# Attention in front of a mixture of experts: score banks with fixed owners, rows turned by two engines, and weight splits one chunk later

## Chip, core and metric

One core of a Trainium2 chip. The metric is the device time of one execution in microseconds; the time before is the median of three runs. Engines are called by their names in the profile: PE (TensorE; PEld its weight loads), DVE (VectorE), ACT (ScalarE), POOL (GpSimd) and SP (SyncE, which here only issues transfers).

## What is computed

Attention over 4 batches of 12 heads, 448 tokens and 64 columns a head, with a tanh cap on the scores; its output, as 1792 rows of 768, goes to a mixture of 8 experts with one expert for each row.

```python
scores = cap * np.tanh(scale * np.matmul(q, k.transpose(0, 1, 3, 2)) / cap)
scores = scores - np.max(scores, axis=-1, keepdims=True)
attn = np.exp(scores)
attn = attn / (np.sum(attn, axis=-1, keepdims=True) + 1e-09)
x = np.matmul(attn, v)                 # -> (1792, 768)
logits = x @ w_gate; e_idx = np.argmax(logits, axis=1)
eom = 1.0 / (1.0 + np.exp(-(x @ w_output_gate)))
for e in range(8):
    mask = e_idx == e
    ye = np.maximum(x[mask] @ w1[e], 0.0) @ w2[e]
    out[mask] = gate_w[mask, None] * eom[mask, e, None] * ye
```

## The kernel before

**Units.** Attention runs over 24 units `u`, six for each batch; a unit is two heads (j = 0, 1, head p and head p + 6). The code is written in the order in which each engine shall work (a manual schedule), so an engine takes its instructions strictly in that order, and the framework adds only the waits. For each unit PE makes the transposed scores in three full tiles of 128 tokens for both heads and a fourth, `s3`, that holds the last 64 tokens of both heads (`qk`). Each is a sum of three products, since Q and K are split in a high plane (`QH`, `K0H` to `K4H`) and a low one (`QL`, `K0L` ...). ACT puts a tanh over each tile (L398) and one exponential over the unit (`expo`, L401). One unit later PE multiplies by V (`pv`, L409, tile `u`), and ACT, or DVE in the first eight units, copies the result to SBUF as `ut` (`u_evac`).

**Sums.** POOL adds the four score tiles (`presum`, tile `pb`); every second unit PE multiplies these by a column of ones (`sums`, L441, tile `sm`).

**K and Q.** SP loads them in blocks of 32 columns; DVE turns the blocks with its 32x32 transpose (`turned`, L290) into a PSUM bank `tk`, and makes the planes by a cast (L280) and a difference (L286). `TURN` says how many of these steps are written before and after the rest of a unit's work; they run about three units ahead of their use. K's last 64 tokens of both heads are split by two extra casts and differences each.

**Banks.** Two banks of PSUM go to transposes and sums. The other six are a ring of three tiles of two banks (`scores`, `half`); whatever PE needs next, a score tile, `u`, or a small product, takes the next one of the three and waits until its last reader is done.

**End of a batch.** `end_of_batch` spreads the work on a finished batch over slots of the units behind it: the gate products (`gate_mm`, tile `tg`), the reciprocals of the sums (`sums_tr`, `recips`), the rows of x (`row_tr` on PE, tile `trow`; `row_out` on DVE, which multiplies by the reciprocals), the choice of the expert and the row's place in the expert's table (`logits`, `choose`, `rank_mm`, `place`, `place2`, `enter`). SP stores the rows (`store_rows`), POOL scatters the table entries. Slot names: "f" and "g" stand behind the unit's scores, "h" behind its exponential, "q" behind pv, "e" at its end.

**Hand-over.** While the last batch is still being finished, `two1` and `two2` start with two blocks of rows that share one expert's weights (`mm_two`): `split_to` splits each weight chunk (`raw`) in a high plane by ACT (L1069) and a low one by DVE (L1070), a fixed number of chunks ahead of PE's use, and then issues the load of the chunk that takes its place. `fetch_dma` loads a block's table rows (`tc`), `gather` fetches its rows of x (`xg`), and `tx` turns them on PE (`pt_x`).

Of the kernel before, what the change touches and what calls it, by code (L numbers as in the profile page):

```python
# [22 lines left out]
def tile_kernel(ctx: ExitStack, tc, q, k, v, cap, w_gate, w_ogate, w1, w2, out):  # L23
# [26 lines left out]
    for i, kind in enumerate((2, 4)):  # L50
# [8 lines left out]
    TURN = {0: (0, 0), 1: (0, 0), 3: (2, 1), 5: (2, 1), 6: (2, 1), 7: (2, 1), 9: (2, 1), 10: (1, 0), 11: (1, 0), 13: (2, 1),  # L59
            14: (2, 1), 15: (2, 1), 17: (1, 0), 20: (1, 0), 21: (0, 0), 22: (0, 0)}  # L60
# [47 lines left out]
    def load_natural(dst, src, n, m, engs):  # L108
        for j in range(2):
            engs[j].dma_start(out=dst[:, 0:n, j], in_=src[j, 0:n * m].rearrange("(c p) d -> p c d", c=n))  # L110

    def load_nat(u, engs):
        (k0, q0), k_, q_ = nat[u], heads(k, u), heads(q, u)
        load_natural(k0, k_, NK, 128, engs)
        engs[1].dma_start(out=k0[0:64, NK], in_=k_[:, SK:S].rearrange("j p d -> p j d"))
        load_natural(q0, q_, NCH, CP, engs)

    def load_pair(src, u, tiles, to):
        t = raw1[tiles[u // 2 % 3]][:, 0:2 * S].rearrange("p (h r a) -> p h r a", h=2, a=32)
        lo = u % 2  # L120
        for c in range(4):
            x = c % 2
            h = c // 2 * NP + u % NP
            nc.sync.dma_start(
                out=t[32 * c:32 * c + 32, lo:].rearrange("p h r a -> p (h r) a"),
                in_=src[u // NP, h:h + 2 - lo, :, 32 * x:32 * x + 32].rearrange("h (r b) a -> b (h r) a", b=32))
        for i in range(lo, 2):
            to[u + i - lo] = t[:, i]

    def load_k(u):  # L130
        load_pair(k, u, (0, 1, 4), ldk)

    def load_q(u):
        load_pair(q, u, (2, 3, 5), ldq)

    def v_main(u, eng):
        load_natural(vvs[u // 2 % 2][:, u % 2], heads(v, u), NK, 128, (eng, eng))

    def v_tails(u, eng):
        for j in range(2):  # L140
            h = j * NP + u % NP
            eng.dma_start(out=vvs[u // 2 % 2][64 * j:64 * j + 64, :, NK, j],
                          in_=v[u // NP, h:h + 2, SK:S].rearrange("h p d -> p h d"))
# [43 lines left out]
    for hl in kpl:  # L187
        for t in hl:
            nc.vector.memset(t.bitcast(F32)[0:64, SK + 64:], 0.0)
            nc.vector.memset(t.bitcast(F32)[64:128, SK:SK + 64], 0.0)  # L190
    for u in range(1, NN):
        load_nat(u, (nc.sync, nc.sync))
# [3 lines left out]
    ohc = rtp.tile([128, NP, 32], F32, name="ohc")  # L196
# [58 lines left out]
    def late_consts():  # L255
        nc.vector.memset(ohc, 0.0)
        for p in range(NP):
            nc.vector.memset(ohc[:, p, p:p + 1], 1.0)
# [29 lines left out]
    def turned(src, n):  # L288
        ps = tbank([128, n], "tk")
        nc.vector.transpose(out=ps, in_=src.rearrange("p r a -> p (r a)"))  # L290
        return ps
# [41 lines left out]
    def t_k(u):  # L333
        pl[u] = planes_of(k_parts(u, turned(ldk.pop(u), S)))
# [39 lines left out]
    def nat_q(u):  # L374
        pq = scores("tq0")[:, 0, 0:S]
        for c in range(NCH):
            nc.tensor.transpose(pq[:, c * CP:(c + 1) * CP], nat[u][1][:, c].rearrange("p j d -> p (j d)"), ident[0:CP, 0:CP])
        return pq

    def qk(u, s):  # L380
        KH, KL, QH, QL = pl[u]
        if s == 0:
            pt[u] = ptp.tile([128, 2 * NK + 1, S], F32, tag="pt", name="pt")
        n = 2 if s < NK else 1
        sl = slice(s * 128, (s + 1) * 128)
        if s < NK:
            ps = scores("s")
            for i, (x, y) in enumerate(((KH, QH), (KL, QH), (KH, QL))):
                for j in range(2):
                    h = slice(64 * j, 64 * j + 64)  # L390
                    nc.tensor.matmul(ps[:, j, 0:S], lhsT=x[h, sl], rhs=y[h], start=(i == 0), stop=(i == 2))  # L391
            ps = ps[:, :, 0:S]
        else:
            ps = half("s3")[:, 0:S]
# [8 lines left out]
    def pv(u, c):  # L403
        P = pt[u]
        V = vvs[u // 2 % 2][:, u % 2]
        if c == 0:
            ups[u] = half("u")[:, 0:S]
# [24 lines left out]
    def sums(u):  # L432

        b, p = divmod(u, NP)
        if p % 2 == 0:
            return
        r = p // 2
        if r == 0:
# [21 lines left out]
    def end_of_batch(b):  # L460
        def bank(shape, name, m=False):
# [4 lines left out]
            x = half(name)[0:shape[0], 0:math.prod(shape[1:])]  # L466
# [5 lines left out]
        def sums_out():  # L472
            ssb = T("ssb", [128, S])
            nc.scalar.activation(out=ssb, in_=smt.pop(b), func=ACTF.Copy)
# [7 lines left out]
        def recips():  # L482
            r = T("rec", [CP, NCH, NP // 2, 4])
            nc.vector.tensor_scalar(out=r.rearrange("p c n j -> p c j n"), in0=rt["trec"][:, :, :, 0:NP // 2],
                                    scalar1=epsc[0:CP], scalar2=None, op0=ALU.add)
            nc.vector.reciprocal(out=r, in_=r)
# [25 lines left out]
        def gate_mul(g):  # L512
            if g == 0:
                T("gm", [CP, NCH, H, 16])
            for i in range(2):
                c = 2 * g + i
                nc.vector.tensor_tensor(
                    out=rt["gm"][:, c], in0=rt["pg"][:, i].rearrange("p (h e) -> p h e", h=H),
                    in1=rec[b][:, c].unsqueeze(2).to_broadcast([CP, H, 16]), op=ALU.mult)

        def logits():
            l = T("lg", [CP, NCH, 16])
# [3 lines left out]
            d = T("d")  # L526
            nc.vector.tensor_tensor(out=d, in0=l[:, :, 0:E], in1=mx.unsqueeze(2).to_broadcast(sh), op=ALU.subtract)

        def choose():

            d = rt["d"]
            cand = T("cand")
            stt(cand, d, 0.0, ALU.is_lt, iota8[0:CP], ALU.add)
            fi = T("fi", [CP, NCH])
# [4 lines left out]
            nc.vector.tensor_tensor(out=og, in0=ohb, in1=rt["lg"][:, :, E:2 * E], op=ALU.mult)  # L539
# [17 lines left out]
        def place():  # L557
            ohb, ps = rt["ohb"], rt["ps"]
            rk = T("rk")
# [6 lines left out]
        def place2():  # L566
            rk = rt["rk"]
            nc.vector.tensor_tensor(out=rk, in0=rk, in1=rt["ohb"], op=ALU.mult)
            nc.vector.tensor_reduce(out=posi, in_=rk, axis=AX.X, op=ALU.max)

        def enter():

            den = rt["den"]
            nc.vector.tensor_reduce(out=den[:, 0], in_=rt["ex"], axis=AX.X, op=ALU.add)
            nc.vector.tensor_scalar(out=den[:, 1], in0=den[:, 1], scalar1=1.0, scalar2=None, op0=ALU.add)
            stt(den[:, 0], den[:, 0], 1e-9, ALU.add, den[:, 1], ALU.mult)
# [37 lines left out]

        L = lambda *fs: (lambda: [f() for f in fs])
        P = lambda f, *a: (lambda: f(*a))
        rws = [L(P(row_tr, p), P(row_out, p)) for p in range(NP)]
# [3 lines left out]
        if b < B - 2:  # L621
            at = {(-2, "q"): [g0], (0, "q"): [g1], (0, "e"): [sums_out], (1, "g"): [t[1]],
                  (2, "g"): [rws[0], rws[1]], (3, "g"): gts, (3, "h"): [logits], (4, "g"): [rws[2], rws[3]], (4, "h"): [choose],
                  (5, "g"): [rank_mm, place, rws[4]], (5, "h"): [place2, enter], (6, "g"): [rws[5]]}
            for i, x in enumerate(((6, "g"), (8, "g"), (9, "g"), (10, "g")) if b == 0 else ((6, "g"),) * NCH):
                at.setdefault(x, []).append(P(scatter, (i,)))
        elif b == B - 2:
# [7 lines left out]
                  (2, "q"): [fd[0], *lds[:2], fd[1]],  # L635
# [342 lines left out]
    for u in range(NU):  # L978
        if u % 2 and u < NU - 3:
            load_v(u + 1)  # L980
        for s in range(NK):
            qk(u, s)
# [4 lines left out]
        else:  # L987
            qk(u, NK)
# [127 lines left out]
    def mm_two(ps, which, acts, n, lag, done):  # L1116
# [250 lines left out]
```

## Time and profile before

| what | value |
|---|---|
| median of 3 runs | 509.56 us (508.12 to 510.07) |
| profiled execution | 510.44 us, span of its instructions 508.8 us |
| mean granted clock of PE | 0.993 |
| PE busy | 488.6 us (96%) |
| DVE busy | 383.0 us (75%) |
| ACT busy | 371.4 us (73%) |
| POOL busy | 286.8 us (56%) |

The busy share is a mean over stages: attention up to about 192 us, where all engines work, the end of the last batch and the first expert blocks up to about 240, and the experts behind them. Matmuls are pipelined and their ends are modelled, so PE's busy share overstates its work; what it waits for is read from the rows of one place in time.

### The profile page before, as it was taken

The page shows a single profiled execution, that of the slowest core. Times are in us where ns is not written, and L with a number is a line of the kernel's source. Part 1 is how long each engine was busy: PE and PEld are TensorE (multiplying, and loading weights), DVE is VectorE, ACT ScalarE, POOL GpSimd, SP SyncE. Part 2 cuts the span into 40 slices and gives each one's busy share as a digit, 9 for nine tenths or more (in the row PEclk, how much of TensorE's full clock was granted, in tenths as well). Part 3 has the DMA queues.
Part 4 walks back from the last instruction along what each step waited for, and adds up shares of the span by engine and source line. Part 5 has one row for each costly group of instructions (what it writes and reads, how often), then busy time and mean ns, then how long its engine had stood idle before and what let it go on. Part 6 is the DMA issues. An engine that isn't in the chain of part 4 may idle for free. (4 is left out here: it accounts for less than half of the span.)

```text
span 508.8 us, 9997 instructions
## 1 busy us (share of the span) xinstructions
PE 488.6 (96%) x3064; PEld 342.2 (67%) x3064; DVE 383.0 (75%) x746; ACT 371.4 (73%) x433; POOL 286.8 (56%) x310
## 2 busy tenths in 40 slices
PE   8999999999999999899999999999999999999994
PEld 6544445454544443678989979978788867686691
DVE  6789998889887879698989868866677947555550
ACT  5999998888978797356688968867677856674551
POOL 7899998698988614562259771237274144522001
PEclk9999999999999999899999999999999999999998
DMA  7879877476431449872199235279679599791001
GB/s 174 138 130 162 154 134 139 89 134 107 78 62 38 83 120 327 301 224 104 26 390 406 82 114 214 63 274 366 219 249 402 200 395 409 215 379 42 1 33 50
DMA packets 152379, 91.92 MB, mean 181 GB/s; under 512 B 135026, under 2 KB 135162, under 8 KB 152320
## 3 DMA queue, kind: packets, MB, share of 16 engines
q1 hardware_dynamic: 142336, 58.24, 42.8%
q0 software_dynamic: 8832, 32.74, 17.7%
q8 instruction: 26, 0.43, 0.3%
q10 hardware_dynamic: 1152, 0.25, 0.2%
q14 instruction: 33, 0.27, 0.2%
HBM read 123.68 MB, written 12.04 MB: 267 GB/s over the span
## 5 line engine op out<-in xcount | busy, mean ns | idle before, releaser
L1070 DVE TENSOR_TENSOR wr<-raw,wr 128x768 fp32r<-128x768 f32 (+1 forms) x167 | 171.9, 1067 | 66.5 <-ACT wr L1069 65.7
L1069 ACT ACTIVATE wr<-raw 128x768 fp32r<-128x768 f32 (+1 forms) x167 | 150.7, 935 | 30.9 <-PE py L1091 15.2
L398 ACT ACTIVATE pt<-s,icap 128x896 f32<-128x896 f32 x96 | 79.9, 913 | 11.0 <-PE s L391 10.8
L409 PE MATMUL u<-pt,vv 128*64 128x448 f32 x384 | 77.5, 546 | 1.4 <-ACT pt L398 1.1
L1091 PE MATMUL py<-wr,hh 128*128 128x384 f32 x352 | 77.3, 341 | 0.0
L1091 PE MATMUL php<-wr,xh 128*128 128x512 f32 x264 | 74.8, 405 | 0.0
L1160 POOL DMA_INDIRECT out_dram<-yo,ti x13 | 21.4, 1648 | 94.5 <-ACT yo L1158 71.3
L401 ACT ACTIVATE pt<-pt,capc 128x3136 f32<-128x3136 f32 x24 | 69.9, 2912 | 0.6
L1091 PEld LDWEIGHTS py<-wr,hh 128*128 128x128 f32 x352 | 61.2, 188 | 4.0 <-issue 3.7
L1091 PEld LDWEIGHTS php<-wr,xh 128*128 128x128 f32 x264 | 47.4, 188 | 12.8 <-issue 2.8
L409 PEld LDWEIGHTS u<-pt,vv 128*64 128x64 f32 x384 | 25.4, 136 | 41.3 <-issue 33.0
L417 POOL TENSOR_TENSOR pb<-pt 128x896 f32<-128x896 f32 x20 | 42.3, 2116 | 14.1 <-ACT pt L401 4.4
L422 POOL TENSOR_TENSOR pb<-pb,pt 64x448 f32<-64x448 f32 x40 | 45.7, 1142 | 3.1
L1091 PE MATMUL py<-wr,hl 128*128 128x384 f32 x176 | 44.8, 335 | 0.0
L418 POOL TENSOR_TENSOR pb<-pb,pt 128x896 f32<-128x896 f32 x20 | 42.0, 2100 | 1.6
L1091 PE MATMUL php<-wr,xl 128*128 128x512 f32 x132 | 41.6, 396 | 1.0 <-DVE xl L886 1.0
L1207 POOL DMA_DIRECT2D rh<-in_moe_w_dram x42 | 23.2, 555 | 16.6 <-DVE wr L1070 8.9
L1091 PEld LDWEIGHTS py<-wr,hl 128*128 128x128 f32 x176 | 31.8, 188 | 0.0
L1091 PEld LDWEIGHTS php<-wr,xl 128*128 128x128 f32 x132 | 24.7, 188 | 7.3 <-DVE xl L886 1.4
L290 DVE STREAM_TRANSPOSE tk<-raw 128x448 f32<-128x448 f32 x42 | 27.5, 655 | 0.9
L585 POOL DMA_INDIRECT tab<-ent,posi x16 | 17.0, 1061 | 13.3 <-DVE ent L577 8.9
L1261 POOL DMA_INDIRECT out_dram<-yh,toh x6 | 6.0, 1007 | 29.8 <-ACT yh L1260 7.4
(315 smaller groups left out, 820.1 us busy)
## 6 DMA issues: line engine op xcount, KB each, us to landing
raw<-in_moe_w_dram SPq DMA_DIRECT2D x78, 512.0 KB
raw<-in_moe_w_dram SPq DMA_DIRECT2D x104, 384.0 KB
rh<-in_moe_w_dram POOLq DMA_DIRECT2D x18, 512.0 KB, 7.1
rh<-in_moe_w_dram POOLq DMA_DIRECT2D x24, 384.0 KB, 8.4
raw<-in_q_dram SPq DMA_DIRECT2D x45, 112.0 KB
vv<-in_v_dram SPq DMA_DIRECT2D x48, 96.0 KB
raw<-in_k_dram SPq DMA_DIRECT2D x40, 112.0 KB
xs<-xr SPq DMA_DIRECT2D x36, 112.0 KB
```

What stands on the lines that cost most here:

```text
L290: nc.vector.transpose(out=ps, in_=src.rearrange("p r a -> p (r a)"))
L398: nc.scalar.activation(out=pt[u][:, 2 * s:2 * s + n], in_=ps, func=ACTF.Tanh, scale=icap)
L401: nc.scalar.activation(out=pt[u], in_=pt[u], func=ACTF.Exp, scale=capc)
L409: nc.tensor.matmul(ups[u][64 * j:64 * j + 64], lhsT=V[:, c, j, :], rhs=P[:, 2 * c + (j if c < NK else 0)], start=(c == 0), stop=(c == NK))
L417: eng.tensor_tensor(out=s1[u], in0=P[:, 0:2], in1=P[:, 2:4], op=ALU.add)
L418: eng.tensor_tensor(out=s1[u], in0=s1[u], in1=P[:, 4:6], op=ALU.add)
L422: eng.tensor_tensor(out=s1[u][h, j], in0=s1[u][h, j], in1=P[h, 2 * NK], op=ALU.add)
L1069: nc.scalar.activation(out=t[:, 0, 0:F], in_=raw, func=ACTF.Copy)
L1070: nc.vector.tensor_tensor(out=t[:, 1, 0:F], in0=raw, in1=t[:, 0, 0:F].bitcast(F32), op=ALU.subtract)
L1091: nc.tensor.matmul(ps[g][:, 0:n], lhsT=st[:, c], rhs=w[:, z, g * n:(g + 1) * n], start=(c == 0 and st is hi and z == 0), stop=(c == (KD, K ...
L1160: nc.gpsimd.indirect_dma_start(out=out, out_offset=bass.IndirectOffsetOnAxis(ap=ti, axis=0), in_=y, in_offset=None, bounds_check=NT - 1, o ...
L1207: nc.gpsimd.dma_start(out=d, in_=rows_of(src, e, w, c), **kw)
```

## The change

- The six banks get fixed owners: score tiles 0 and 2 share A (two banks), tile 1 has B, the fourth tile C (one bank), `u` has D. Small products take the first half of B and C in turn. From the third unit on the tiles are made in the order 0, 1, fourth, 2.
- In batches 0 and 1 four rows of six (`BYV`) are turned by DVE's block transpose instead of PE (`row_v`, with the reciprocals in that layout from `recips_b`), and stored in four pieces of 32 columns. The slots are dealt out anew.
- `sums` makes 64 output rows for each head instead of 32, so that one product serves both layouts. The small epsilon is added by ACT as it copies the sums.
- K's tail is its first 64 tokens for one head and its last 64 for the other, and the K tiles hold zeros in the gaps, so that a turned K block is 512 columns and is split by one cast and one difference. Its loads go head by head.
- Small tiles of the choice (`lgd`, `rkb`, `dex`) lie in PSUM for batches 0 to 2; two gate products become one.
- `mm_two` splits one chunk less ahead, and the first weight chunk is loaded ahead of the first table rows.

```diff
-    ring = [0]
-    def scores(name):
-        ring[0] += 1
-        return ps_s.tile([128, 2, 512], F32, tag=f"s{ring[0] % 3}", name=name)
-    def half(name):
-        return scores(name)[:, 0]
+    def scores(name, z):
+        return ps_s.tile([128, 2, 512], F32, tag="AB"[z], name=name)
+    def single(name, z):
+        return ps_s.tile([128, 512], F32, tag="CD"[z], name=name)
+    spare = [0]
+    def extra(name):
+        spare[0] ^= 1
+        return scores(name, 1)[:, 0] if spare[0] else single(name, 0)
...
-        for g in range(4):
-            nc.tensor.matmul(smt[b][32 * g:32 * g + 32], lhsT=ohc[:, r, :], rhs=s1[u - 1 + g // 2][:, g % 2],
-                             start=(r == 0), stop=(r == NP // 2 - 1))
+        for v in (u - 1, u):
+            z = v % NP
+            for j in range(2):
+                nc.tensor.matmul(smt[b][64 * j:64 * j + 64], lhsT=ohc[:, NP - 1 - z:NP + 63 - z], rhs=s1[v][:, j],
+                                 start=(z == 0), stop=(z == NP - 1))
...
+            nc.vector.transpose(out=ps[:, 0:SK], in_=src[:, 2:14].rearrange("p r a -> p (r a)"))
+            nc.vector.transpose(out=ps[:, SK:].rearrange("p (n k) -> p n k", n=2),
+                                in_=src.rearrange("p (n r) a -> p n (r a)", r=2)[:, 0::7])
...
+        if u >= NN:
+            return [hi, lo], [(hi, lo, ps)]
...
+    def load_k(u):
+        t = kview[u // 2 % 3]
+        for i in range(u % 2, 2):
+            for c in range(4):
+                j, x = divmod(c, 2)
+                nc.sync.dma_start(
+                    out=t[32 * c:32 * c + 32, i, 2 * j:2 * j + 14],
+                    in_=blocks(k[u // NP, j * NP + u % NP + i - u % 2], x).rearrange("(r b) a -> b r a", b=32))
...
+        def row_v(p):
+            nrow[0] += 1
+            ps = tbank([128, S], "tkr")
+            nc.vector.transpose(out=ps, in_=ut[b * NP + p])
+            x = xrp.tile([128, NCH * 128], F32, tag=f"xr{nrow[0] % 3}", name="xr")[:, 0:S].rearrange("p (t m) -> p t m", m=32)
+            nc.vector.tensor_tensor(out=x, in0=ps.rearrange("p (t m) -> p t m", m=32),
+                                    in1=rt["recb"][:, p].unsqueeze(2).to_broadcast([128, NB, 32]), op=ALU.mult)
...
-            rk = T("rk")
+            rk = rt["rk"] = small("rkb", sh) if b < B - 1 else T("rk")
...
-            at = {(-2, "q"): [g0], (0, "q"): [g1], (0, "e"): [sums_out], (1, "g"): [t[1]],
-                  (2, "g"): [rws[0], rws[1]], (3, "g"): gts, (3, "h"): [logits], (4, "g"): [rws[2], rws[3]], (4, "h"): [choose],
-                  (5, "g"): [rank_mm, place, rws[4]], (5, "h"): [place2, enter], (6, "g"): [rws[5]]}
+            at = {(-2, "q"): [g0], (0, "q"): [g1], (0, "e"): [sums_out], (1, "g"): [t[1], rws[0]], (1, "e"): [recips_b],
+                  (2, "e"): [rws[1], rws[2]], (3, "g"): gts, (3, "e"): [rws[3]], (4, "h"): [logits, choose],
+                  (5, "g"): [rank_mm, place, place2, rws[4]], (5, "h"): [enter], (6, "e"): [rws[5]]}
...
-                  (2, "q"): [fd[0], *lds[:2], fd[1]],
+                  (2, "q"): [lds[0], fd[0], lds[1], fd[1]],
...
-        for s in range(NK):
+        for s in range(NK) if u < NN else (0, 1, NK):
             qk(u, s)
...
-                w[c] = next_planes((which + 4, 0, c), RB - lag)
+                w[c] = next_planes((which + 4, 0, c), RB - lag - 1)
```

Line numbers behind the change are higher by 25 to 63; the rows below carry those of their own kernel.

PE's queue in unit 9, before: two score tiles, the fourth tile, two rows, pv, the sums.

```order
L391 MATMUL s<-QL,K4H 128x448 x2
L396 MATMUL s_1066<-QH,K4H 128x448
L396 MATMUL s_1066<-QH,K4L 128x448
L396 MATMUL s_1066<-QL,K4H 128x448
L594 MATMUL trow<-ident,ut 112x128 x8
L409 MATMUL u<-pt,vv_120 64x448 x8
L441 MATMUL sm<-pb,ohc 32x448 x4
```

The same place after:

```order
L421 MATMUL s_1052<-QL,K4H 128x448
L416 MATMUL s<-QH,K4H 128x448 x2
L416 MATMUL s<-QH,K4L 128x448 x2
L416 MATMUL s<-QL,K4H 128x448 x2
L434 MATMUL u<-pt,vv_120 64x448 x8
L467 MATMUL sm<-pb,ohc 64x448 x4
```

The fourth tile has moved ahead of the third, the two rows are gone from in front of pv, and the sums are 64 wide.

DVE's queue at the hand-over, before: the low part of the second block (`xl`), the split of the next expert's first chunk (`raw_0`), then the last batch's reciprocals.

```order
L886 TENSOR_TENSOR xl<-pt_x,xh 128x512
L886 TENSOR_TENSOR xl<-pt_x,xh 128x256
L1070 TENSOR_TENSOR wr<-raw_0_106,wr 128x1024
L484 TENSOR_SCALAR rec<-trec,epsc 112x4x4x3
L486 RECIPROCAL rec<-rec 112x48
L517 TENSOR_TENSOR gm<-pg,rec 112x192 x2
L599 TENSOR_TENSOR xr<-trow,rec 112x512
```

After:

```order
L947 TENSOR_TENSOR xl<-pt_x,xh 128x512
L947 TENSOR_TENSOR xl<-pt_x,xh 128x256
L1132 TENSOR_TENSOR wr<-raw_5_111,wr 128x1024
L510 RECIPROCAL rec<-trec 112x4x2x6
L540 TENSOR_TENSOR gm<-pg,rec 112x384
L634 TENSOR_TENSOR xr<-trow,rec 112x512
L1132 TENSOR_TENSOR wr<-raw_0_106,wr 128x1024
```

The split of `raw_0` has moved behind the reciprocals and the first row; the chunk in front of them, `raw_5`, is the last one of the expert at work.

## Rows read from the trace of the kernel before

**Rows 1.** Busy time by stretch: PE, PEld, DVE, ACT, POOL, clock, DMA share, GB/s.
```profile
260.00:280.00 20.00, 20.00 (x110) 18.04 (x109) 17.82 (x20) 16.41 (x22) 14.45 (x18) 1.00 1.02 397
```
**Rows 2.** Timeline from unit 4 to unit 5: start us, busy us, instruction, idle before.
```profile
40.97 3.30 ACT L398 ACTIVATE pt<-s,icap 128x896 f32<-128x896 f32 x4
43.17 3.23 PE L409 MATMUL u<-pt,vv 128*64 128x448 f32 x16
46.33 0.96 PE L441 MATMUL sm<-pb,ohc 128*32 128x448 f32 x8
47.10 0.93 PE L495 MATMUL tg<-ut,wg 128*32 128x448 f32 x6
47.96 0.47 PE L391 MATMUL s<-QH,K1H 64*128 64x448 f32 x2
48.94 3.33 ACT L398 ACTIVATE pt<-s,icap 128x896 f32<-128x896 f32 x4 [0.31 <-PE s L391]
```
**Rows 3.** Timeline of unit 11, where two rows are turned on PE.
```profile
85.81 3.33 ACT L398 ACTIVATE pt<-s,icap 128x896 f32<-128x896 f32 x4 [0.29 <-PE s L391]
89.25 3.23 PE L409 MATMUL u<-pt,vv 128*64 128x448 f32 x16
95.03 3.52 ACT L398 ACTIVATE pt<-s,icap 128x896 f32<-128x896 f32 x4
```
**Rows 4.** Timeline, the exponentials of unit 7 and of unit 18.
```profile
58.45 2.91 ACT L401 ACTIVATE pt<-pt,capc 128x3136 f32<-128x3136 f32 x1
...
147.63 2.91 ACT L401 ACTIVATE pt<-pt,capc 128x3136 f32<-128x3136 f32 x1
```
**Rows 5.** Timeline at the hand-over, in order of time.
```profile
207.76 2.01 ACT L1069 ACTIVATE wr<-raw 128x1024 fp32r<-128x1024 f32 x2 [3.00 <-DMA raw<-in_moe_w_dram]
208.85 1.23 DVE L1070 TENSOR_TENSOR wr<-raw,wr 128x1024 fp32r<-128x1024 f32 x1 [3.31 <-ACT wr L1069]
210.34 0.55 PE L510 MATMUL pg<-ident,gsb 96*112 96x96 f32 x4 [0.86 <-DVE rec L484]
212.16 1.10 PE L594 MATMUL trow<-ident,ut 128*112 128x128 f32 x4 [1.27 <-DVE xr L599]
```
**Rows 6.** Busy time by stretch at the hand-over, columns as in rows 1.
```profile
210.00:212.00 2.00, 0.55 (x4) 0.35 (x4) 1.86 (x6) 0.00 (x0) 0.00 (x0) 0.95 1.02 412
212.00:214.00 2.00, 1.84 (x7) 1.65 (x8) 2.00 (x5) 0.00 (x0) 1.53 (x2) 0.50 0.38 133
214.00:216.00 2.00, 2.00 (x10) 1.61 (x9) 1.94 (x3) 0.37 (x1) 1.34 (x2) 0.70 0.89 285
```
**Rows 7.** Groups by line and form on DVE, 20 to 170 us.
```profile
L290 DVE STREAM_TRANSPOSE tk<-raw 128x448 f32<-128x448 f32 x42 | 27.5, 655 | 0.9
L599 DVE TENSOR_TENSOR xr<-trow,rec 112x512 f32<-112x512 f32 x15 | 10.1, 689 | 6.3 <-PE trow L594 6.2
L280 DVE CAST K3H<-tk 128x384 fp32r<-128x384 f32 x5 | 2.8, 558 | 0.2
L280 DVE CAST K3H<-tk 64x64 fp32r<-64x64 f32 x10 | 2.2, 216 | 0.2
```
**Rows 8.** Single lines: duration ns min/median/max, first and last start us.
```profile
L568 DVE TENSOR_TENSOR rk<-rk,ohb x4: 173/918/1064, 99.4 to 228.8; 112x32 f32<-112x32 f32 x4
L564 DVE TENSOR_TENSOR rk<-pre,trk x4: 180/180/180, 98.3 to 221.8; 112x32 f32<-112x32 f32 x4
```
**Rows 9.** Single lines on SP's queue, columns as in rows 8.
```profile
L124 SPq DMA_DIRECT2D raw<-in_k_dram x44: 426/542/2169, 12.1 to 122.4; - x44
L606 SPq DMA_DIRECT2D xs<-xr x36: 304/490/1734, 78.0 to 179.0; - x36
```
**Rows 10.** Timeline of the first block's table rows, its gather and its turn.
```profile
184.37 2.14 SPq L857 DMA_DIRECT2D tc<-tab  x4
190.16 1.14 POOL L872 DMA_INDIRECT xg<-xs,ti  x1 [0.71 <-POOL ti L865]
195.33 0.87 PE L884 MATMUL pt_x<-ident,xg 128*128 128x128 f32 x6
```

More of the change, by code (lines that the diff above doesn't have):

```diff
@@ L193, in tile_kernel @@
     load_v(0)
-    ohc = rtp.tile([128, NP, 32], F32, name="ohc")
+    ohc = rtp.tile([128, NP + 63], F32, name="ohc")
     wg = rtp.tile([128, NP, 2, 16], F32, name="wg")
@@ L256, in late_consts @@
         nc.vector.memset(ohc, 0.0)
-        for p in range(NP):
-            nc.vector.memset(ohc[:, p, p:p + 1], 1.0)
+        nc.vector.memset(ohc[:, NP - 1:NP + 32:32], 1.0)
         for g in range(4):
@@ L374, in nat_q @@
     def nat_q(u):
-        pq = scores("tq0")[:, 0, 0:S]
+        pq = (scores("tq0", 1)[:, 0] if u == 2 else single("tq0", 1))[:, 0:S]
         for c in range(NCH):
@@ L406, in pv @@
         if c == 0:
-            ups[u] = half("u")[:, 0:S]
+            ups[u] = (single("u", 1) if u < NU - 1 else scores("u", 1)[:, 0])[:, 0:S]
         for j in range(2):
@@ L465, in bank @@
                 return ps_m.tile(shape, F32, tag="sm", name=name)
-            x = half(name)[0:shape[0], 0:math.prod(shape[1:])]
+            x = extra(name)[0:shape[0], 0:math.prod(shape[1:])]
             if len(shape) == 2:
@@ L514, in gate_mul, with small @@
                 T("gm", [CP, NCH, H, 16])
[L515 to L519, printed above, removed]
-        def logits():
-            l = T("lg", [CP, NCH, 16])
+            cs = slice(2 * g, 2 * g + 2)
+            nc.vector.tensor_tensor(
+                out=rt["gm"][:, cs], in0=rt["pg"].rearrange("p i (h e) -> p i h e", h=H),
+                in1=rec[b][:, cs].unsqueeze(3).to_broadcast([CP, 2, H, 16]), op=ALU.mult)
+        def small(nm, shape):
+            n = math.prod(shape[1:])
+            return tbank([CP, n], nm).rearrange("p (c e) -> p c e", c=shape[1])
+        def logits():
+            if b < B - 1:
+                w = rt["lgd"] = small("lgd", [CP, NCH, 16 + E + 1])
+                l, d = w[:, :, 0:16], w[:, :, 16:16 + E]
+            else:
+                l, d = T("lg", [CP, NCH, 16]), T("d")
             nc.vector.tensor_reduce(out=l, in_=rt["gm"].rearrange("p c h e -> p c e h"), axis=AX.X, op=ALU.add)
@@ L566, in place2 @@
         def place2():
[L567 to L568 removed]
+            y = rt["rk"]
+            rk = T("rk") if b < B - 1 else y
+            nc.vector.tensor_tensor(out=rk, in0=y, in1=rt["ohb"], op=ALU.mult)
             nc.vector.tensor_reduce(out=posi, in_=rk, axis=AX.X, op=ALU.max)
@@ L597, in row_out @@
             nrow[0] += 1
-            x = xrp.tile([CP, NCH, 128], F32, tag=f"xr{nrow[0] % 3}", name="xr")
+            x = xrp.tile([128, NCH * 128], F32, tag=f"xr{nrow[0] % 3}", name="xr")[0:CP].rearrange("p (c m) -> p c m", c=NCH)
             nc.vector.tensor_tensor(
@@ L613, in row_out, with recips_b, store @@
                 stores.append(store)
+        NB = S // 32
+        BYV = (1, 2, 3, 5) if b < B - 2 else ()
+        def recips_b():
+            ps = tbank([128, S], "tks")
+            nc.vector.transpose(out=ps, in_=rt["ssb"])
+            r = T("recb", [128, NP, NB])
+            nc.vector.reciprocal(out=r, in_=ps.rearrange("p (t r) -> p r t", r=32)[:, 0:NP])
+        def row_v(p):
[5 more added lines that the diff above has]
+                                    in1=rt["recb"][:, p].unsqueeze(2).to_broadcast([128, NB, 32]), op=ALU.mult)
+            def store():
+                for a in range(4):
+                    m0 = D * (p + a // 2 * NP) + 32 * (a % 2)
+                    nc.sync.dma_start(
+                        out=xs[b * S:(b + 1) * S, m0:m0 + 32].rearrange("(t i) m -> i t m", i=32),
+                        in_=x[32 * a:32 * a + 32])
+            stores.append(store)
         L = lambda *fs: (lambda: [f() for f in fs])
         P = lambda f, *a: (lambda: f(*a))
-        rws = [L(P(row_tr, p), P(row_out, p)) for p in range(NP)]
+        rws = [P(row_v, p) if p in BYV else L(P(row_tr, p), P(row_out, p)) for p in range(NP)]
         t = [sums_out, L(sums_tr, recips), L(P(gate_mm, 0), P(gate_out, 0)), L(P(gate_mm, 1), P(gate_out, 1))]
@@ L987, in tile_kernel @@
         else:
-            qk(u, NK)
+            qk(u, NK if u < NN else 2)
         if u == 0:
```

85 lines of the change are left out of this document (48 added, 37 removed).

## The prediction

> **What bounds the kernel now.** I read the busy times by stretch first. In the stage of the experts TensorE (PE) is busy 20.00 of 20 us [rows 1], and so on in every such stretch up to 460 us. So the change, which touches attention and the hand-over to the experts, can only move the start of that full stretch; behind it nothing is rearranged.
>
> In attention I read one turn of the loop, from the first tanh of a unit to that of the next. In the turn that starts at 40.97 ScalarE's (ACT) tanhs take 3.30 us and PE begins the value product (pv) 2.20 us after the first of them, at 43.17. It takes 3.16 us until the sums start, the sums 0.77 until the gate product (tg), which is busy 0.93; the next first tanh comes at 48.94, 7.97 us after the last [rows 2]. The reader is to see that PE's work behind the tanhs closes the circle: whatever delays pv, and whatever stands between pv and the next scores, is paid once per unit. From the first score matmul at 47.96 to that tanh, one score tile and a handshake, are 1.0 us. ACT's own floor is the tanhs plus the exponential of 2.91, 6.2 us, and some 0.5 more with the copy of u that it makes from unit 8 on. Where rows of the output are turned on PE, pv starts later: in unit 11 at 89.25, 3.44 us after the tanh at 85.81, and the turn takes 9.22 [rows 3]. The 11 turns from the exponential of unit 7 to that of unit 18 take 89.18 us together [rows 4].
>
> At the hand-over I read who waits for whom in time. ACT waits 3.00 us for a weight chunk, VectorE (DVE) 3.31 us for ACT's split of it, and the reciprocals, which need neither, stand behind that split in DVE's queue. PE then waits 0.86 us for them and 1.27 us for the row tile behind them [rows 5]. [...]
>
> **The change, part by part.** *Fixed score banks and the order 0, 1, 3, 2.* The third score tile now waits for the first tanh (1.0 us) and takes about 0.75 itself (the 1.0 us from 47.96 to 48.94 less the handshake), so pv may start 1.8 us after the first tanh instead of 2.2, since it no longer waits for the second tanh's bank. A plain turn is then 1.8 + 3.16 + 1.0 = 6.0 us, under ACT's floor of 6.2 to 6.7.
>
> *Sums for both heads of a row.* Four matmuls 32 columns wide, running side by side, become four that are 64 wide, of pv's shape: two at a time. pv has eight of them in 3.16 us [rows 2], so four cost 1.55 instead of 0.77: +0.78 us in each odd unit from 3 on.
> [...]
>
> *Rows.* In batches 0 and 1 four of six rows leave PE: two of them put pv at 3.44 us instead of 2.20, so 0.6 us each with their bank waits [rows 2, 3]. DVE pays a transpose of 0.655 and a product of about 0.63 for a product of 0.689 [rows 7], +0.6 us eight times.
>
> So by units 7 to 17, where T is the first tanh. 7: 1.8 + 3.16 + 1.55 + 0.93 + 1.0 = 8.4. 8: sums' transpose and one row on PE before pv, 7.1. 9: 7.5. 10: gate transposes, 7.0. 11: 8.4. 12: rank and a row, 7.05. 13: as 7, plus copies of u and of the sums on ACT, 8.85. 14 to 17 as 8 to 11: 7.1, 7.5, 7.0, 8.4. Sum 84.3 against 89.18 [rows 4]: **-4.9 us**. Outside these, units 3 and 5 have the longer sums and only 0.3 to 0.4 us of earlier pv, +0.9 with unit 1 and 2's unchanged order; from unit 18 on the longer sums of units 19, 21 and 23, and three rows in a line that find two banks where three stood, **+1.8 us** in all. Attention: **-2.2 us**, bounds -6 (the sums all hidden under ACT) and +3 (the sums all paid, no wait saved).
>
> *VectorE's other edits.* The K block goes from one transpose, three casts and three differences, 0.655 + 2 x (0.558 + 2 x 0.216) = 2.64 us, to two transposes and one cast and one difference of 512 columns. With 1.07 ns a column from the 384 and 64 column casts [rows 7] these are 0.59, about 0.3 and 2 x 0.69, 2.3 us. The merged gate product, and the epsilon that rides on ACT's copy, save about 0.6 us a batch. A batch of DVE then costs about 41 us, as before, against 45 us of turns. That cover is thin: DVE makes planes three units ahead, and if it is gone each microsecond over 45 is paid.
> *Small tiles in PSUM.* The product that places a row, 0.173 us alone, took 0.918 in the median [rows 8]; in the trace the slow ones lie under a GpSimd addition. With one operand in PSUM I take 0.18, the time of the operation that already reads PSUM [rows 8]: some 5 us of DVE in three batches, none of it on the path.
> [...]
>
> *Loads and stores on SyncE's queue.* K comes in eight transfers for a pair of units instead of four, and a row turned by DVE leaves in four pieces instead of two: 24.7 issues for two units in the row stage instead of 18. At the median of 0.542 us for K and 0.490 for stores [rows 9] that is about 13.5 us of 15. Loads run about six units ahead, which hides it. Bytes and K's packets stay the same.
>
> *Hand-over.* The first weight chunk is now fetched ahead of the first table rows. These were issued at 184.37, and the gather that they lead to at 190.16; PE turns what it brought at 195.33, just as pv ends [rows 10]. One register load and one issue more delay the gather by about 1.3 us. What lies late next is the turn of x. Against it, DVE gets the chunk earlier. Bounds -1 and +1.5; I take **+0.7 us**, nearer the delay because that row has no slack.
>
> *Later splits.* The split of the next expert's chunk moves behind the reciprocals. PE's two waits, 0.86 + 1.27, and the slow clock, 1.84 x 0.5 + 2.00 x 0.3 = 1.5 us [rows 5, 6], go: **-3.6 us**, bounds 0 and -4. The chunk itself belongs to the expert behind the pair that PE works on, so its lateness stays hidden.
>
> Startup has 12 small memsets for 20, and six on the K tiles: nothing, since PE waits for the first loads there.
>
> **Sum:** -2.2 + 0.7 - 3.6 = -5.1 us on the profiled execution's 510.44 (span 508.8): 505.3. That execution lies 0.9 above the median of 509.56, so the prediction is **504.5 us**. Within 0.5%, 2.5 us, this kernel's measurement can't tell a change from none.
>
> **Rivals.**
> (1) *No change, 508 to 511.* The splits are moved but PE then stops for something else in the same place, because the transfers are full there (412 GB/s in 210 to 212 [rows 6]), and the later gather costs 1.5 us. Then -2.2 + 1.5 - 1 = -1.7, or 507.9, and 510 with half of the attention gain. For it: share of the transfers 1.02. Against: nothing that PE does for the pair needs the late chunk.
> (2) *Slower, 512 to 516: SyncE's queue becomes the pace in units 8 to 17.* The gain is gone when five pairs at 24.7 issues exceed 15.0 us by 5.1 in all, at 0.65 us an issue; at 0.70 they cost 11.5 us and the kernel 516. For it: maxima of 2.169 and 1.734 in the rows, and that stores wait in this queue ahead of V. Against: medians of 0.54 and 0.49 [rows 9] and the six units of lead.
> (3) *VectorE becomes the pace there, 507.* If a batch takes 43 us and comes in lumps (units 9, 11, 13 hold 7.3 to 8.2 us of it), PE waits for the banks of gate and rows, and half of the 4.9 is gone: about 507. For it: 41 of 45 us. Against: the three units of lead.
>
> **How the numbers follow.** Forecast 0.57, (1) 0.20, (2) 0.13, (3) 0.10. The forecast's own range is 501 to 507; some of (1) and (2) spreads above and the attention bound of -6 below, so the range is 498.5 to 511, which leaves out most of (2) and a little of the rest. Faster by over 0.5%: nearly all of the forecast and half of (3), 0.61; the same: 0.23; slower: 0.16.
>
> **What would show it.** In the new profile pv starts 1.8 us after the first tanh in plain units, and turns of odd units last 7.5 or 8.4 us. The sums take 1.55 us to the next work on PE. From exponential 7 to 18 there are 84 us. No drop of the clock after the first expert's third chunk, and the reciprocals directly behind a split that has no wait. The placing product takes 0.18 us in all batches. PE waits at the first turn of x for the gather, up to 1.5 us. I am wrong if SyncE's queue shows issues of over 0.65 us back to back and DVE waits for K, if PE's score tiles wait for DVE, or if the stall at 210 us comes back with another name.

## The result, and the profile after

The changed kernel takes **513.96 us** (median of 7 runs, 511.08 to 515.71) against 509.15 (7 runs, 508.12 to 510.07): ratio 1.0081, 95% interval 1.0063 to 1.0099. It is slower, outside my range. Ratios here and below leave out runs more than 1.5% above the fastest of their kernel, which takes four of ten from run 4 and none from the others. The profiled execution is the one of 513.96, with a span of 512.4 us against 508.8.

I first laid marks along both traces; the sign says how far the new kernel is behind the old at each.

| start of, us | before | after | behind |
|---|---|---|---|
| exponential of unit 2 | 25.00 | 28.20 | +3.2 |
| of unit 7 | 58.45 | 63.57 | +5.1 |
| of unit 18 | 147.63 | 149.65 | +2.0 |
| of unit 23, the last | 189.21 | 193.81 | +4.6 |
| first turn of x on PE | 195.33 | 201.53 | +6.2 |
| third turn of x | 221.09 | 222.98 | +1.9 |
| end of the span | 508.8 | 512.4 | +3.6 |

Four stretches lose (the start, the units outside 7 to 18, the first gather, and one behind the third turn of x), two win (units 7 to 18, and the hand-over behind the first turn of x). The timeline of the new kernel on ACT, exponentials of units 2, 7, 18 and 23:

```profile
28.20 2.91 ACT L426 ACTIVATE pt<-pt,capc 128x3136 f32<-128x3136 f32 x1
...
63.57 2.91 ACT L426 ACTIVATE pt<-pt,capc 128x3136 f32<-128x3136 f32 x1
...
149.65 2.92 ACT L426 ACTIVATE pt<-pt,capc 128x3136 f32<-128x3136 f32 x1
...
193.81 2.91 ACT L426 ACTIVATE pt<-pt,capc 128x3136 f32<-128x3136 f32 x1
```

Units 7 to 18 take 86.08 us where they took 89.18 [rows 4]: a gain, 1.8 us less than forecast.

The start, timeline of unit 1, and then PE's busy time in stretches of 2 us (busy, granted clock, share of the transfers, GB/s):

```profile
16.43 0.47 PE L416 MATMUL s<-QH,K1H 64*128 64x448 f32 x2 [1.73 <-ACT pt L423]
...
17.54 1.01 ACT L423 ACTIVATE pt<-s,icap 128x896 f32<-128x896 f32 x1 [0.26 <-PE s L416]
...
19.62 2.91 ACT L426 ACTIVATE pt<-pt,capc 128x3136 f32<-128x3136 f32 x1
20.58 0.60 PE L434 MATMUL u<-pt,vv 128*64 128x448 f32 x2
```

```profile
14.00:16.00 2.00, 0.71 (x8) 1.00 0.74 121
16.00:18.00 2.00, 1.56 (x8) 0.74 0.36 55
18.00:20.00 2.00, 2.00 (x8) 0.50 0.70 112
20.00:22.00 2.00, 2.00 (x12) 0.91 0.67 108
```

The reader is to see a stop and what follows it. In units 0 to 2 the tiles still go in the order 0, 1, 2 (the new order begins with unit 3, the fourth), but tiles 0 and 2 now share a bank pair. So PE stops for 1.73 us until the tanh of tile 0 has read it, and right behind that stop its granted clock is at 0.50 for three us, from 17 to 20. The slow stretch that stood at 212 to 216 [rows 6] is gone from there; this one is new.

A turn with sums and the start of a plain one, PE and ACT:

```profile
33.52 3.23 PE L434 MATMUL u<-pt,vv 128*64 128x448 f32 x16
...
36.58 1.67 PE L467 MATMUL sm<-pb,ohc 128*64 128x448 f32 x8
38.18 0.47 PE L416 MATMUL s<-QH,K4H 64*128 64x448 f32 x2
...
39.15 3.33 ACT L423 ACTIVATE pt<-s,icap 128x896 f32<-128x896 f32 x4 [1.42 <-PE s L416]
...
41.21 3.23 PE L434 MATMUL u<-pt,vv 128*64 128x448 f32 x16
...
44.37 0.47 PE L416 MATMUL s<-QH,K0H 64*128 64x448 f32 x2
```

The sums hold PE for 1.60 us (36.58 to 38.18); pv starts 2.06 us behind the first tanh, not 1.8. From 38.18 to 44.37, where the scores behind that pv begin, PE works 6.19 us without a gap, as much as ACT's own floor of 6.2: nothing is hidden under ACT any more.

The first gather: POOL, the chunk loads on SP, and PE.

```profile
193.92 1.91 SPq L895 DMA_DIRECT2D raw<-in_moe_w_dram  x4
194.13 1.28 POOL L933 DMA_INDIRECT xg<-xs,ti  x1 [0.36 <-DMA raw<-in_moe_w_dram]
...
196.87 3.18 PE L434 MATMUL u<-pt,vv 128*64 128x448 f32 x16
...
201.53 0.87 PE L945 MATMUL pt_x<-ident,xg 128*128 128x128 f32 x6 [1.48 <-DMA xg<-xs,ti]
```

From issue to PE's turn it takes 7.40 us, and PE waits 1.48 (its weight load, whose record begins earlier, 2.26); it took 5.17, with PE just done, before [rows 10]. Four chunk loads are issued next to it.

Behind it, where the old stall was [rows 5], ACT's splits start without a wait, and the reciprocals stand directly behind a split that hardly waits:

```profile
210.39 2.00 ACT L1131 ACTIVATE wr<-raw 128x1024 fp32r<-128x1024 f32 x2
...
211.48 1.23 DVE L1132 TENSOR_TENSOR wr<-raw,wr 128x1024 fp32r<-128x1024 f32 x1 [0.19 <-ACT wr L1131]
212.62 0.45 DVE L510 RECIPROCAL rec<-trec 112x48 f32<-112x48 f32 x1
212.91 0.49 PE L534 MATMUL pg<-ident,gsb 96*112 96x96 f32 x4
```

And one place far in the experts' stage, of which I had written that nothing is rearranged there:

```profile
397.96 0.85 ACT L1131 ACTIVATE wr<-raw 128x768 fp32r<-128x768 f32 x1 [3.00 <-DMA raw<-in_moe_w_dram]
...
400.76 0.66 PE L945 MATMUL pt_h<-ident,h 128*128 128x128 f32 x4 [1.04 <-ACT hth L1000]
```

ACT waits for a late chunk, the half block's copy `hth` stands behind that split, and PE waits for it: the marks move from +1.9 to +3.2 us here.

### The profile page after: what moved, and what is told of

It is laid out like the page before. It is cut to its first block, busy times and chain, and to the rows that moved or that the text cites. A ratio compares the mean times of both kernels' runs of the same rounds, so it can differ in the third digit from the quotient of the medians.

```text
span 512.4 us, 9924 instructions
## 1 busy us (share of the span) xinstructions
PE 493.6 (96%) x3032; PEld 340.8 (67%) x3032; DVE 380.7 (74%) x679; ACT 370.9 (72%) x433; POOL 296.9 (58%) x310
## 3 DMA queue, kind: packets, MB, share of 16 engines
q1 hardware_dynamic: 150400, 58.24, 44.0%
## 5 line engine op out<-in xcount | busy, mean ns | idle before, releaser
L423 ACT ACTIVATE pt<-s,icap 128x896 f32<-128x896 f32 (+1 forms) x96 | 80.5, 914 | 16.6 <-PE s L416 15.4
L933 POOL DMA_INDIRECT xg<-xs,ti x14 | 18.9, 1347 | 6.1 <-POOL ti L926 3.5
```

The lines of the kernel that those rows point to most:

```text
L933: nc.gpsimd.indirect_dma_start(out=g, out_offset=None, in_=xs[0:n], in_offset=bass.IndirectOffsetOnAxis(ap=ti, axis=0), bounds_check=n - 1 ...
```

## The experiments

All are compared with the kernel before, run on the same chip (medians 509.0 to 509.4). A cause is read from the marks, since the medians of the kernels with the two-tile start spread by several us.

**1. The splits undone.** Edit: `RB - lag - 1` back to `RB - lag`.

> The changed kernel with one edit: the splits of the pair's weights are again made as far ahead as before. Theory (the later splits are the part that worked: from the second turn of x to the third the new kernel is 3.9 us ahead of the old): the stall in front of the reciprocals and the slow clock come back, 3.6 to 3.9 us slower than the changed kernel, about 517.7 us, and the rows show PE waiting for the reciprocals or the row behind a split. Rival (what was won there came from the later start of the loads or from the order of the first chunk, not from the splits): within 1 us of the changed kernel, 513 to 515, and no such wait.

Measured 514.89 us (4 runs, 513.78 to 515.81), ratio 1.0115. That is 0.9 us over the changed kernel by the medians; the intervals of the two ratios (1.0092 to 1.0139 and 1.0063 to 1.0099) overlap. The theory falls: between the last exponential and the third turn of x lie 28.86 us, against 29.17 in the changed kernel and 31.88 before. The split stands in front of the reciprocals again, and does no harm:

```profile
212.85 1.06 ACT L1131 ACTIVATE wr<-raw 128x1024 fp32r<-128x1024 f32 x1
...
213.94 1.23 DVE L1132 TENSOR_TENSOR wr<-raw,wr 128x1024 fp32r<-128x1024 f32 x1 [0.19 <-ACT wr L1131]
215.08 0.45 DVE L510 RECIPROCAL rec<-trec 112x48 f32<-112x48 f32 x1
215.37 0.49 PE L534 MATMUL pg<-ident,gsb 96*112 96x96 f32 x4
```

The split for which ACT waited until 207.76 before [rows 5] starts at 212.85 without a wait. This profile also shows the clock fall once more, behind a stop of PE of 1.42 us, from 173.11 to 174.53, for a bank that DVE had not read:

```profile
172.00:174.00 2.00, 1.11 (x9) 1.00 0.89 172
...
176.00:178.00 2.00, 2.00 (x9) 0.50 0.53 72
```

**2. The tables first again.** Edit: `(2, "q"): [fd[0], *lds[:2], fd[1]]`.

> The changed kernel with one edit: the first table rows are again loaded ahead of the first weight chunk. In the changed kernel PE waits 2.26 us for the first gathered block, whose transfer takes 7.4 us where it took 5.1 us before. Theory (the one issue and the register load in front of the table rows cost it 1.25 us, and the gather then meets the chunk loads): the gather is issued 1.2 to 1.6 us earlier against the last exponential, PE's wait falls under 0.9 us, and the kernel gains 1 to 1.6 us, about 512.6. Rival (the gather is slow because five chunk loads are issued next to it, whatever stands first): the wait stays at 2 us and the time within 0.5 us, 513.5 to 514.5.

Measured 512.3 us (4 runs, 510.14 to 515.4), 1.0089 (1.0054 to 1.0124). The median fits the theory, the ratio shows no gain over 1.0081, and the rows don't fit: the gather is issued at 191.49, 0.66 us earlier against the last exponential, takes 7.77 us, and PE still waits 1.19 (1.48). The profiled run, 510.14, owes its time to something else: its start had the 1.73 us stop but no slow clock, so that its third exponential came at 26.25, and it lacks the loss at 400 us, 1.6 us behind the third turn of x. So the gather goes with the rival, and the 1.7 us of the median are not shown to come from this edit.

**3. Three tiles under way at the start.** In units 0 and 1 (also in the edit, not printed: the tanh of that tile in two halves, and Q's transposes for unit 1, moved to tile 1's banks):

```diff
-            ps = scores("s", s % 2)
+            three = u < 2 and s == 2
+            if three:
+                pj = [single("s", z) for z in range(2)]
+            else:
+                ps = scores("s", s % 2)
+                pj = [ps[:, z] for z in range(2)]
...
-            ps = single("s3", 0)[:, 0:S]
+            ps = (scores("s3", 0)[:, 0] if u < 2 else single("s3", 0))[:, 0:S]
```

> The changed kernel with one edit: in units 0 and 1 the third score tile takes the two single banks (two tanhs of half the size, so 0.25 us more on ACT each) and the fourth tile the bank pair of the first, so that three tiles are under way as before. Theory (the shared pair A lets PE stop for 1.7 us in unit 1, and its granted clock then drops to 0.50 for three us; together with unit 2 this is 3.2 us by the third exponential): the third exponential starts near 25.5 instead of 28.2, no clock drop before 30 us, and the kernel is 2.5 to 3 us faster, about 511.2. Rival (the first units are late for their loads, and K's new tail transfers are what is slow): the third exponential stays above 27.5 and the time within 1 us.

Measured 510.1 us (10 runs, 509.2 to 514.16), 1.0036. The start is cured; the clock fell at another stop, PE's wait for the gather (timeline rows, then one stretch):

```profile
24.82 2.91 ACT L435 ACTIVATE pt<-pt,capc 128x3136 f32<-128x3136 f32 x1
...
198.18 0.88 PE L954 MATMUL pt_x<-ident,xg 128*128 128x128 f32 x6 [2.00 <-DMA xg<-xs,ti]
```

```profile
200.00:202.00 2.00, 2.00 (x7) 0.50 0.97 245
```

The third exponential is 3.4 us earlier, and the kernel faster by 3.9 us in the median, 2.3 by the ratios, whose intervals (1.0013 to 1.0059 and 1.0063 to 1.0099) don't meet.

**4. Narrow sums, all rows on PE.** The four sums side by side as before, `BYV = ()`, the rows in "g" slots.

> The changed kernel with two edits that go together: the sums are 32 wide again (four side by side), and all rows are turned on PE. Theory (PE's queue is full in attention, so every microsecond that it is given is paid): the narrow sums give back 0.78 us in each of 11 units, 8.6 us; the eight rows that return to PE cost 0.55 to 0.65 us each, 4.4 to 5.2 us, and some waits for banks. Net 2.5 to 4 us faster, about 510.5, nearly all of it in batches 2 and 3, where no row was taken from PE. Rival (the turns are set by ACT and the banks, and the sums are hidden): the turns of odd units keep their length, the rows' cost comes on top, and the kernel is 2 to 4 us slower, 516 to 518.

Measured 511.88 us (504.76 to 513.99), 1.0016, interval 0.998 to 1.0052. As a time it is not clear, and the median of all ten is above the 510.5 that I expected: the times go roughly with the mean granted clock, 504.76 and 508.08 at 0.996, 511.63 at 0.988. The marks are: the last exponential comes at 186.96, 6.85 us earlier. Of this 2.2 us are a start without slow clock (third exponential at 26.00); 4.65 are the edit, somewhat more than expected. The sums now hold PE 0.89 us in place of 1.60:

```profile
34.49 0.96 PE L467 MATMUL sm<-pb,ohc 128*32 128x448 f32 x8
35.38 0.47 PE L416 MATMUL s<-QH,K4H 64*128 64x448 f32 x2
...
196.35 0.88 PE L956 MATMUL pt_x<-ident,xg 128*128 128x128 f32 x6 [3.20 <-DMA xg<-xs,ti]
```

The turns of units 18 to 23 take 41.22 us in place of 44.16, units 2 to 7 34.02 in place of 35.37; 7 to 18, where the rows come back, only 85.72 in place of 86.08. The marks bear the theory out: what wide sums cost there, four rows taken off PE give back.

**5. The later splits alone, in the kernel before.** Edit: `RB - lag` to `RB - lag - 1`.

> The kernel before with the later splits alone. Undoing them in the changed kernel did not bring the stall back: there the chunk had landed when its split came up. Theory (the stall of the kernel before is a chunk that lands late, and the splits in front of the reciprocals carry it to PE): with the splits later, PE's waits of 0.86 and 1.27 us and the slow clock behind them go, and the kernel is 2 to 3.6 us faster, 505.5 to 507. Rival (transfers are full there, so what isn't paid at the reciprocals is paid a little later at the chunk itself): third turn of x within 0.7 us of where it was, time 508 to 509.5.

Measured **506.16 us** (6 runs, 505.42 to 507.44), ratio 0.9941 (0.9921 to 0.9961). The theory holds. ACT's wait is still there, but what stands behind it now hurts nobody:

```profile
206.16 0.30 DVE L484 TENSOR_SCALAR rec<-trec,epsc 112x48 f32<-112x48 f32 x1
206.43 0.49 PE L510 MATMUL pg<-ident,gsb 96*112 96x96 f32 x4
...
207.37 2.01 ACT L1069 ACTIVATE wr<-raw 128x1024 fp32r<-128x1024 f32 x2 [2.38 <-DMA raw<-in_moe_w_dram]
```

**6 to 8. The cures together.** The cure of the gather puts the third block's table rows ahead of the chunks:

```diff
-                  (3, "h"): [P(gather, 0), P(gather, 1), *lds[2:KD]],
-                  (3, "e"): [fd[2], *lds[KD:KD + 2], fd[3]], (4, "f"): lds[KD + 2:]}
+                  (3, "h"): [P(gather, 0), P(gather, 1), fd[2], *lds[2:KD]],
+                  (3, "e"): [*lds[KD:KD + 2], fd[3]], (4, "f"): lds[KD + 2:]}
```

Run 6 is run 4 with this edit. Run 7 adds the start of run 3, and lets unit 2 go in the order 0, 1, 3, 2. Run 8 is the changed kernel with both cures, the start as in run 7, and, in batches 2 and 3 alone (`if b >= B - 2`), the narrow sums.

> The run with narrow sums and all rows on PE, with one more edit: the table rows of the third block are issued ahead of chunks 2 to 5 of the first expert, so that these chunks reach the queues 2 us later, behind the first gather. Theory (in the changed kernel the gather takes 7.4 us and not 5.1 because chunk loads are issued in front of it): the gather takes 5 to 6 us, PE's wait for it falls from 3.2 us to 1.5 or less, and the median falls from 511.9 to 507 to 509, more than the wait alone since PE's clock drops less often behind it. Rival (it is the gather's own start that is late, and held chunks are missing later): the wait moves to a chunk, time within 1 us of 511.9.

Measured 509.33 us (506.24 to 510.22), 1.0001 (0.9981 to 1.0021): 2.5 us better than run 4 by the medians, 0.8 by the ratios, whose intervals overlap, so the gain in time is not clear. The marks are: the gather is issued at 191.20 and PE turns its rows at 195.16 without a wait. Against the last exponential the first turn of x comes 3.21 us earlier than in run 4, but the third only 1.43, and ACT waits 2.30 us for the split at 208.03, which the rival foresaw.

> The last kernel with the start cured too: in units 0 and 1 three tiles under way, unit 2 in the new order of tiles. Theory (the prices add up: 2.5 to 3 us of the start, 2.3 to 3 us of the gather, 3 to 4 us of the sums): third exponential near 25, last near 185, median 504 to 506.5, below both kernels. Rival (what attention wins waits at the hand-over, since the chunks land when they land): the last exponential is 3 us earlier, but PE's waits between 190 and 220 grow by as much, median 507 to 509.

Measured **505.87 us** (504.73 to 508.11), 0.9935 (0.9912 to 0.9958). It beats both kernels, but theory and rival each have half: the last exponential comes at 185.51, 3.65 us earlier than in the kernel before with the later splits; the third turn of x at 215.98 is 1.01 earlier. Of the 2.64 us lost between them, 1.57 fall before the second turn, where PE waits 0.83 and 0.41 us for the first two gathers, and 1.07 behind it, where ACT's split is late again and PE waits for a row that stands behind it:

```profile
206.47 2.01 ACT L1151 ACTIVATE wr<-raw 128x1024 fp32r<-128x1024 f32 x2 [3.55 <-DMA raw<-in_moe_w_dram]
...
209.90 0.65 PE L649 MATMUL trow<-ident,ut 128*112 128x128 f32 x4 [1.04 <-DVE xr L654]
```

> The changed kernel with the start and the gather cured, rows on DVE kept in batches 0 and 1 with the wide sums that they need, narrow sums in batches 2 and 3 only. Theory (a row taken from PE and the wide sums cancel: 4 x 0.6 us against 3 x 0.75 us a batch): within 1 us of the run with all rows on PE and narrow sums, the exponentials from unit 7 to 18 within 0.7 us of it, median 504.5 to 507. Rival (rows on PE cost more, by their bank waits): 2 us faster than that run.

Measured **505.6 us** (6 runs, 504.8 to 505.99), 0.9928 (0.9909 to 0.9947), the fastest, and within the error of runs 5 and 7. Units 7 to 18 take 84.73 us against 85.73 with all rows on PE, units 2 to 7 34.98 against 33.61: the first stretch is 1.0 apart where I expected 0.7 at most, and the two add to 119.7 and 119.3, so rows on DVE with wide sums and rows on PE with narrow ones cost nearly the same.

**9. The splits undone in that kernel.** Edit as in run 1.

> The last of the cured kernels (start and gather cured, narrow sums late, rows on DVE) with the splits as far ahead as before. In the changed kernel undoing the later splits brought no stall back; in the kernel before, making them later won 3 us. Theory (it depends on when the pair gets there: there the second turn of x came at 211 us, when the chunk had landed; here it comes at 200, as in the kernel before at 203): ACT waits for a chunk again, PE waits for the reciprocals or a row, and the kernel is 2 to 3.5 us slower, 507.6 to 509. Rival (the new order of loads or the shorter chain of reciprocals keeps the stall away): within 1 us of 505.6.

Measured 508.91 us (507.68 to 510.95), 0.9997 (0.9981 to 1.0013): 3.3 us slower than run 8, as the theory has it.

```profile
205.75 0.65 PE L520 MATMUL trec<-ident,ssb 128*112 128x128 f32 x4 [1.43 <-DVE xl L967]
...
207.51 2.01 ACT L1151 ACTIVATE wr<-raw 128x1024 fp32r<-128x1024 f32 x2 [2.39 <-DMA raw<-in_moe_w_dram]
...
211.52 0.65 PE L649 MATMUL trow<-ident,ut 128*112 128x128 f32 x4 [0.72 <-DVE xr L654]
```

**10. The gather's cure alone, in the changed kernel.**

> The changed kernel with the one edit of the gather: the third block's table rows are issued ahead of chunks 2 to 5, so that these reach the queues behind the first gather. Theory (chunk loads in front of it are what slows the gather): it takes 4 to 5.8 us in place of 7.4, PE waits under 0.8 us for it, and the kernel gains 1.5 to 2.3 us, about 512. Rival (the pair gets there late anyway, and the time is made up for by chunks that have landed): the wait goes, but the third turn of x keeps its distance from the last exponential, 29 us, and the time is 513.5 to 514.5.

Measured 511.17 us (10 runs, 509.4 to 516.21), 1.0053 (1.0021 to 1.0085): 2.8 us better than the changed kernel by the medians, 1.4 by the ratios, whose intervals overlap. The first turn of x starts as pv ends, and the third comes 28.2 us behind the last exponential, 1.0 nearer than in the changed kernel; the first turn comes 1.55 nearer. So part of the win is given back on the way, as the rival says. The chunks now stand behind the gather, and ACT waits for its split again, 2.31 us:

```profile
193.55 1.28 POOL L933 DMA_INDIRECT xg<-xs,ti  x1 [0.36 <-DMA tc<-tab]
...
195.90 3.58 SPq L895 DMA_DIRECT2D raw<-in_moe_w_dram  x6
196.30 3.18 PE L434 MATMUL u<-pt,vv 128*64 128x448 f32 x16
...
211.87 2.01 ACT L1131 ACTIVATE wr<-raw 128x1024 fp32r<-128x1024 f32 x2 [2.31 <-DMA raw<-in_moe_w_dram]
```

## Why the prediction was wrong

The sum was attention -2.2, hand-over +0.7, later splits -3.6. On the profiled executions it came to +4.6 up to the last exponential, +1.6 at the gather, -4.3 from the first to the third turn of x, +1.3 at 400 us and some +0.4 behind: +3.6.

**The start: the step that failed most.** I wrote "Startup has 12 small memsets for 20 ...: nothing", and put units 0 to 2 down with "unchanged order". The order is unchanged, the banks are not: a ring let three tiles be under way, fixed owners let two. Price 3.2 us by the third exponential, about 1.2 for the stop (third exponential at 26.0 to 26.25 where the clock held) and 2 for the clock. Run 3 shows it.

**Banks.** In plain turns the forecast gain isn't there. pv starts 2.06 us behind the first tanh and not 1.8: the third tile begins 1.26 us behind it and not 1.0, since the fourth stands in front, and takes 0.80 (40.41 to 41.21). And the 2.20 that I took for a plain turn before, that of unit 5 [rows 2], is not one: in units 2, 3, 4, 6 and 7 pv already started 1.93 to 1.96 us behind the first tanh, as in unit 4:

```profile
34.78 3.33 ACT L398 ACTIVATE pt<-s,icap 128x896 f32<-128x896 f32 x4 [0.72 <-PE s L391]
...
36.74 3.23 PE L409 MATMUL u<-pt,vv 128*64 128x448 f32 x16
```

No run undid the order or the banks of the later units alone. The 1.8 us by which 84.3 became 86.08 are 0.16 for each of eleven turns; they were not taken apart.

**Sums.** Predicted 1.55, measured 1.60. What I under-counted is where they are paid: units 2 to 7 lose 1.9 us where I had +0.9 for everything before unit 7, units 18 to 23 lose 2.6 for 1.8, with 1.2 and 1.4 us of PE's waits for the copy of the sums and for a bank among them. From pv to the sums it takes 3.06 us for 3.16 [rows 2]; why is not shown.

**Rows and VectorE.** As predicted: a K block is 0.59 + 0.33 + 2 x 0.69, 2.3 us; a row on DVE 0.66 + 0.63; PE's matmuls wait for no plane between 20 and 180 us. The placing product (line statistics, as in rows 8) lost its slow cases, and costs 18 ns more from PSUM, 0.191 us against 0.173, where I had taken 7 [rows 8]:

```profile
L602 DVE TENSOR_TENSOR rk<-rkb,ohb x3: 191/191/192, 103.7 to 169.4; 112x32 f32<-112x32 f32 x3
L602 DVE TENSOR_TENSOR rk<-rk,ohb x1: 173/173/173, 231.3 to 231.3; 112x32 f32<-112x32 f32 x1
```

**SyncE's queue, the rival on the side that came true.** Its range, 512 to 516 us, holds the result, but that is luck: its mechanism is not there. K's issues are shorter than before (0.478 us in the median, 0.542 before [rows 9]), and DVE waits for none of them. Only from 170 us on does DVE wait for stores of rows, three times, by 0.49 to 0.78 us, and PE's wait of 1.42 us for a bank at 174.79 stands behind one of them.

```profile
L132 SPq DMA_DIRECT2D raw<-in_k_dram x84: 401/478/1536, 12.1 to 127.0; - x84
```

**Hand-over.** I predicted +0.7 from one issue in front of the table rows; it was 1.6, by something else. The register load and the issue in front of the table rows do hold SyncE, for 1.46 us (185.20 to 186.66). Against the last exponential the gather was issued 0.63 us earlier than before, not later, and took 2.23 us longer. With the first of four chunk loads issued from 0.2 to 1.7 us ahead of it the gather took 7.2 to 8.0 us in five profiles (the changed kernel and runs 1 to 4), and with the chunks behind it 4.1 us in run 7 and at most 5.9 in the other six (the kernel before and runs 5, 6, 8, 9 and 10). How the chunk loads slow it is not shown.

**Later splits.** -3.6 was right for the kernel for which I read it: alone they give 3.0 us (run 5), and 3.3 in the cured kernel (run 9). In this change the marks show nothing from them: the first to the third turn of x take 21.45 us with them and 21.42 without (run 1). The wait that they take out of the way isn't there.

That wait I had also read wrongly: it is not for data. The load of this chunk is conditional (`cond` in `load_raw`) and moves something only where a block's expert differs from that of the block before. SyncE's issues on the load's line in the kernel before, first the six real loads, then this one and the five behind it (ns min/median/max, first and last start):

```profile
L834 SPq DMA_DIRECT2D raw<-in_moe_w_dram x6: 332/333/1113, 202.0 to 205.4; - x6
L834 SPq DMA_DIRECT2D raw<-in_moe_w_dram x6: 73/73/96, 207.7 to 210.0; - x6
```

In the trace of the kernel before the semaphore of the first of the six real loads goes up in sixteen steps, 2.43 to 3.18 us behind its issue, and that of this load in a single step, 0.07 us behind it; in the changed kernel it is a single step after 0.07 us too. The profile counts 81.8 MB of such loads (78 of 512 KB, 104 of 384 KB), while no queue on it moved more than 58.24 MB: some loads moved nothing, and by these signs this was one of them. So ACT waits for SyncE's queue to get to the load, which was at 204.7 to 211.8 us, by kernel (207.66 in the kernel before, where the split starts at 207.76). In the five profiles with the chunk loads ahead of the first gather (the changed kernel, runs 1 to 4) ACT comes later than that and does not wait; in the seven with them behind it (the kernel before, runs 5 to 10) it waits 2.30 to 3.55 us. Run 10, whose attention is as late as the changed kernel's, has the wait again by that one edit.

So the failed step here is that I added this term to the others: it presupposed the old order of gather and chunk loads at the hand-over. What took the wait away also made the gather slow, and run 10 undoes both with one edit; the 4.3 us from the first to the third turn are the stall gone, not a gain of the splits. Why SyncE is ahead of the gather in this kernel stays open; run 2, with the old order of its first loads, has it too.

**At 400 us.** A wait of this kind stands in the profiles of the changed kernel and of run 4 (1.07 us), smaller ones in runs 8 and 10 (0.56 and 0.27 us), none elsewhere. Here the chunk is a real load, issued at 385.34 in the changed kernel and landed at 397.88. What makes it late was not settled.

## What to carry to other kernels

A wait that the profile puts down to a transfer need not be one for data: look at the issue, how long it took and when its queue came to it. And such a term holds only for the order of loads in which it was read: before adding it up, ask which of the two will be there first in the new kernel. Giving banks fixed owners is a change of how many tiles may be under way, and is to be counted where the order of work is *not* changed too. And an edit that takes work from a full engine is worth what the engine must do for it in return: here four rows against three wide sums, next to nothing. The one-line edit of run 5 alone gives as much, within the error, as all the rest with its cures.

## What the hardware showed unexpectedly

At the hand-over ACT waited for a load that by the signs above moved nothing, until SyncE's queue had issued it: 2.30 to 3.55 us in seven profiles. The same stop of 1.7 us at the start was followed by a granted clock of 0.50 for some 3 us in four of six profiles (the changed kernel, runs 1, 6 and 10) and by none in two (runs 2 and 4); all four kernels with three tiles under way (runs 3, 7, 8 and 9) kept 1.00 there. In run 4 a wait of 3.20 us for the gather left the clock at 1.00, in run 3 one of 2.00 us did not. So in these profiles a short stop of PE cost more than its own length now and then, at the start some 2 us (third exponential at 28.20 against 26.00 and 26.25); what decides it is not shown. That kernels with fewer stops also have the narrower times, 511.1 to 515.7 for the changed kernel and 504.8 to 506.0 for run 8, fits this, but run 3 spread from 509.2 to 514.2 with the start cured.
